# Query projection of an attention kernel: the first product of a query pair one slot earlier, the output projection's slots set around the seven products

## The chip, the cores and the metric

The kernel runs on one core of one Trainium2 chip. The time is the device time of one execution in microseconds (us), and of several timed runs the median is taken. A separate execution was taken by the profiler; its rows give the durations used below.

The engines are named as in the profile: PE is TensorE (matrix products), PEld its weight loads, DVE is VectorE, ACT is ScalarE, SP issues the DMAs. Each engine runs its own instructions in order, and semaphores hold an instruction until another engine has done its part.

## What is computed

Inputs in bfloat16: x is 2048 x 512, the caches hold 32 heads of 2048 keys and values of 128 each. Cut to what matters:

```
xn = layernorm(x)
q  = (xn @ wq), split into 32 heads of 128
p  = softmax(q @ k_cache^T / sqrt(128)), per head
s  = concat(p @ v_cache) @ wo
g  = silu(mlp(xn))          # two gelu stages, shifts, residual
out = x + s * g
```

The change lies in q and in the last product with wo.

## The kernel before, in words

**Units and slots.** After a head of about 100 us for the MLP, the attention runs as 128 units. A unit u is one head (of a group of 4) with one block of 512 queries, in the order group, query block, head in the group. A unit has 8 slots, one for each two key chunks of 128, so slot n of the program is unit n // 8, slot n % 8. The loop over n (line 921 on) writes the order out by hand. In each slot PE gets

- **S**: two products of 512 columns, scores of two key chunks into one of two PSUM tiles `ps_s` (`s_slot`, line 412). ACT then takes exp of both, 128x1024, into `pT` (line 423, "exp" below). The S of slot n needs the exp of slot n-2, because there are two `ps_s` tiles.
- **PV**: two products of 512 columns, weights times values, for the slot 10 earlier (`pv_slot`), into `ps_o`.
- at most one or two **fillers**: a piece of the output projection or of the next units' queries.

**The output projection.** `wo_slot` gives PE one product of 512 columns (`ps_wo`, "wo" below) for one of the 4 heads of a group; four of them make a tile of 128 tokens, and part 4, `wo_post` (line 544), lets DVE add the tile to `sacc` (line 560 in most units), which frees the one `ps_wo` buffer. The list `at_wo` (line 965) says in which slots of a unit the five parts stand. It holds for units 14 to 123 and depends on u % 4.

**The queries.** Units 16 to 125 get their queries in pairs (v, v+1): the two heads' projections of a query block are made from seven products of half size instead of eight, and sums of them. Each product, numbered 1 to 7, is two matmuls of 256 columns (`product`, line 363; "P1" to "P7" below). The pair v is made during the units v-2 (even, "the even unit") and v-1 ("the odd unit"); there are 55 pairs, with even units 14, 16, ..., 122. Products 1, 6 and 2 share one PSUM bank `ps_q` and stand in the even unit; 7, 5, 4 and 3 stand in the odd unit in the same bank, opened anew. In between:

- `q_take` 0 (line 393): ACT copies product 1 to `tq` right after product 1, in the order of ACT behind the exp of the same slot. P6 writes the other half of the same bank, and its first matmul waits for this copy.
- `q_part` 0 (line 400): DVE adds P6 and the copy. `q_take` 1 (line 393): ACT writes the first quarter of the queries behind P2. `q_part` 1, 2, 3 (lines 403, 405, 407): DVE sums of the odd unit; P4 waits for line 405, and the next pair's P1 needs the bank that line 407 reads last.

The table of lines 892 to 895 sets the slots: each (k, n) puts product k at slot n, counted from the even unit's first slot.

**Other DVE work of a unit**: sums over `pT` (lines 429, 434), folds (438, 442), the row sum from a transposing DMA (472), the division of `ps_o` (496), and in some units sums of weights for the coming pairs (361).

Of the kernel before, what the change touches and what calls it, by code (L numbers as in the profile page):

```python
# [17 lines left out]
def kernel(  # L18
# [296 lines left out]
    def q_mm(u, dcs, tag="xa"):  # L315
        g, qt, hh = units[u]
        if dcs[0] == 0:
            st[u] = dict(psq=psX.tile([P, 512], FP32, tag=tag, name="ps_q"))
        for dc in dcs:
            mm(st[u]["psq"][:], wqs[g * HG + hh][:, dc, :],  # L320
               xnT[:, dc, qt * 512:(qt + 1) * 512], dc == 0, dc == DC - 1)
# [73 lines left out]
    def q_part(v, i):  # L395
        s = sw[v]
        ps, t = s["ps"], lambda: pS.tile([P, 256], FP32, tag="tq", bufs=3, name="tq")
        if i == 0:
            s["u"] = t()
            pin(nc.vector.tensor_tensor(out=s["u"][:], in0=ps[:, 1, :], in1=s["m1"][:], op=ALU.add))  # L400
        elif i == 1:
            s["u3"] = t()
            pin(nc.vector.tensor_tensor(out=s["u3"][:], in0=ps[:, 0, :], in1=s["u"][:], op=ALU.add))
        elif i == 2:
            pin(nc.vector.tensor_tensor(out=s["q"][:, 3, :], in0=ps[:, 1, :], in1=s["u3"][:], op=ALU.add))
        else:
            pin(nc.vector.tensor_tensor(  # L407
                out=s["q"][:, 1:3, :], in0=ps[:], in1=s["u"][:].unsqueeze(1).to_broadcast([P, 2, 256]),
                op=ALU.add))
            del sw[v]  # L410

    def s_slot(u, p):
        g, qt, hh = units[u]
        s = st[u]
        sps = psS.tile([P, 2, 512], FP32, name="ps_s")
        for j in range(2):
            kc = 2 * p + j
            kv = kTs[g * HG + hh].rearrange("d (i p j) -> d i j p", p=P, j=KJ)
            mm(sps[:, j, :], kv[:, kc // KJ, kc % KJ, :], s["qT"][:], True, True)
        if p % 2 == 0:  # L420
            s.setdefault("pT", []).append(pB.tile([P, 4, 512], BF16, tag="pT", bufs=6, name="pT"))
        jj = 2 * (p % 2)
        pin(nc.scalar.activation(  # L423
            out=s["pT"][-1][:, jj:jj + 2, :], in_=sps[:], func=ACT.Exp, scale=SCALE))
# [7 lines left out]
    def add_next(u, i):  # L432
        a = st[u]["acc"]
        pin(nc.vector.tensor_tensor(out=a[:], in0=a[:], in1=st[u]["pT"][i][:], op=ALU.add))  # L434

    def fold(u):
        a = st[u]["acc"]
        pin(nc.vector.tensor_tensor(out=a[:, 0:2, :], in0=a[:, 0:2, :], in1=a[:, 2:4, :], op=ALU.add))  # L438

    def fold_last(u):  # L440
        a = st[u]["acc"]
        pin(nc.vector.tensor_tensor(out=a[:, 0, :], in0=a[:, 0, :], in1=a[:, 1, :], op=ALU.add))  # L442
# [22 lines left out]
    def turn(u):  # L465
        st[u]["tT"] = pB.tile([P, 4, P], BF16, tag="tT", bufs=2, name="tT")
        pin(nc.sync.dma_start_transpose(out=st[u]["tT"][:], in_=st[u]["acc"][:, 0, :]))

    def turned_sums(u):
        s = st[u]  # L470
        sm = s["sm"] = smp.tile([P, 4], FP32, name="sm")
        pin(nc.vector.tensor_reduce(out=sm[:], in_=s["tT"][:], axis=mybir.AxisListType.X, op=ALU.add))  # L472

    def turned_recip(u):
        s = st[u]
        sm = s["sm"]
        rc = smp.tile([P, 4], FP32, name="rc")
        pin(nc.vector.reciprocal(out=rc[:], in_=sm[:]))
        s["dr"] = drp.tile([P, 4], FP32, name="dr")
        pin(nc.sync.dma_start(out=s["dr"][:], in_=rc[:]))  # L480

    def bcast(u):
        st[u]["rb"] = pB.tile([P, 512], FP32, tag="rb", bufs=2, name="rb")
        pin(nc.sync.dma_start(
            out=st[u]["rb"][:], in_=st[u]["dr"][:].rearrange("p j -> (p j)").partition_broadcast(P)))
# [54 lines left out]
    def pay():  # L540
        while owed:
            y_out(*owed.popleft(), nc.sync)
# [317 lines left out]
    def pv_run(n):  # L860
        while pv_at[0] <= n - LAG:
            pv_slot(*divmod(pv_at[0], SPU))
            pv_at[0] += 1

    def norm_queue(u):
        norm(u)
        gg, qq, hh = units[u]
        if hh == HG - 1:
            wo_todo.extend((gg, 4 * qq + ts) for ts in range(4))
            if gg == NG - 1 and qq not in LATE:  # L870
                fin_load(4 * qq)
# [3 lines left out]
    def wo_slot(part, n, each=2, **kw):  # L875
        gg, t = wo_todo[0]
        if part < HG // each:
            wo_mm(gg, t, tuple(range(part * each, (part + 1) * each)), **kw)
            return
        wo_todo.popleft()  # L880
        wo_post(gg, t, n)
        if gg == NG - 1 and t % 4 < 3 and t + 1 not in fin and t // 4 not in LATE:
            fin_load(t + 1)
# [5 lines left out]
    first, third = {}, {}  # L889
    for v in pairs:  # L890
        a = (v - 2) * SPU
        for k, n in ((1, 1), (6, 2), (2, 5), (7, 8), (5, 9), (4, 12), (3, 13)):
            steps[a + n].append((product, v, k))
        for i, n in enumerate((1, 5)):
            steps[a + n].append((q_take, v, i))
        steps[a + 14].append((q_part, v, 3))
        first[v - 2] = v
        third[v - 1] = (v,)

    def fold_at(u):  # L900
        return 1 if u in third else 0

    def run_steps(n, which):
        for fn, v, k in steps.get(n, ()):
            if fn is which:
                fn(v, k)
# [4 lines left out]
    for h in range(HG, H, 2):  # L911
        u = (h // HG) * QT * HG + (-4, -2)[h % HG // 2]
# [8 lines left out]
    for n in range(UB * SPU):  # L921
        u, p = divmod(n, SPU)
        extra = len(wo_todo) > 1 and u in (2 * HG, 2 * HG + 1)
        if p == 0 and wo_box:
            wo_slot(4, n, each=1)
        s_slot(u, p)
        pv_run(n)
        for v, dcs in q_plan.get(n, ()):
            q_mm(v, dcs)
        run_steps(n, product)  # L930
        run_steps(n, q_take)
        if p == 0 and 1 <= u:
            if u - 2 in TURN:
                turned_sums(u - 2)
                turned_recip(u - 2)
            add_next(u - 1, 3)
        if p == 1 and u - 2 in TURN:
            bcast(u - 2)
        if p == fold_at(u) and 1 <= u:
            for v in third.get(u, ()):  # L940
                q_part(v, 1)
            fold(u - 1)
            for v in third.get(u, ()):
                q_part(v, 2)
            if u != UA and u not in first:
                fold_last(u - 1)
        if p == 2 and u in first:
            q_part(first[u], 0)
            fold_last(u - 1)
        if p == 3 and u - 1 in TURN:  # L950
            turn(u - 1)
        if p == 0:
            twice = extra
        if twice and p < 3:
            wo_slot(p, n, tag="xa")
        for v, k in ((u + 1, 3), (u + 2, 7)):
            if p == k and "psq" in st.get(v, ()) and (k == 3) == (v > FIRST):
                q_copy(v)
        if u - 2 in TURN:
            norm_p, sum_p, wo_p, each = 7, 5, 3, 1  # L960
        else:
            norm_p, sum_p, wo_p, each = 4, 5, 4, 1
        at_wo = [wo_p + i for i in range(HG // each + 1)]
        if FIRST - 2 <= u < LAST:
            at_wo = ([0, 3, 4, 6, 7], [0, 2, 3, 6, 7], [3, 4, 5, 6, 7], [0, 2, 3, 6, 7])[u % 4]
        if p == norm_p and 2 <= u and not u - 2 in TURN:
            norm_queue(u - 2)
        if p == sum_p and 1 <= u and u - 1 not in TURN:
            sums(u - 1)
        if p == sum_p + 1 and 1 <= u and u - 1 not in TURN:  # L970
            bcast(u - 1)
        if u == UA and p in (1, 2, 3):
            wo_slot(p - 1, n)
            if p == 3:
                fold_last(u - 1)
        if p in at_wo and wo_todo and pS is not None and (p == at_wo[0] or wo_box):
            wo_slot(at_wo.index(p), n, each=each)
        if p == norm_p and u - 2 in TURN:
            norm_queue(u - 2)
        run_steps(n, q_part)  # L980
        if p == 4:
            add_first(u)
        if p == 6:
            add_next(u, 2)
        pay()
        held_mm(n)
        for fn in todo.pop(n, ()):
            fn()
        if pS is None and not held:
            right.close()  # L990
            pS = right.enter_context(pool("pS", side="right", reuse_waits="tile"))
# [3 lines left out]
    n = UB * SPU  # L995
# [156 lines left out]
```

## Time and profile before

| | |
|---|---|
| timed runs, median of 3 | 1241.74 us (1241.14 to 1241.91) |
| the profiled execution | 1240.9 us |
| its span, first to last instruction | 1239.1 us |
| DVE busy, ACT busy | 1030.3 us, 1112.6 us |
| weight loads busy | 644.2 us |
| granted PE clock | 1.0 over the whole span |

The span is 1.8 us shorter than the profiled execution's own time, which lies 0.84 us under the median of the timed runs. A row of the timeline has start, length, engine, line of the kernel, operation, written and read tiles, sizes and count; a bracket at its end gives the idle time before it and what ended that. Matmuls overlap in the rows (a matmul of 512 columns has 0.38 us, and the next one starts much earlier), so PE is read from one start to the next, not from lengths.

### The profile page before, as it was taken

What the parts mean: (1) busy time and instruction counts of PE and PEld (TensorE: products, weight loads), DVE (VectorE), ACT (ScalarE), POOL (GpSimd) and SP (SyncE); (2) the same over time, 40 slices, a digit from 0 to 9 for tenths busy, and PEclk for the clock granted to TensorE, in tenths of its full rate; (3) what the DMA queues carried; (4) which work ended last, traced back from release to release, by engine and by line L of the source; (5) the groups of instructions that cost most, each with busy time, mean ns of one, the idle gap of its engine ahead of it and who ended that gap; (6) DMA issues with size and microseconds to landing.
All of it is one profiled execution on the core that took longest, in us unless ns stands there. A gap on an engine that the chain in (4) does not pass through costs nothing.

```text
span 1239.1 us, 17537 instructions
## 1 busy us (share of the span) xinstructions
PE 1233.0 (100%) x6267; PEld 644.2 (52%) x6267; DVE 1030.3 (83%) x1647; ACT 1112.6 (90%) x1237; POOL 26.7 (2%) x75
## 2 busy tenths in 40 slices
PE   9999999999999999999999999999999999999998
PEld 6444444455555555555555555555555555555555
DVE  7712778898888888888889888888889999999997
ACT  6345999899999999999999999999999999999996
POOL 5300000000000000000000000000000000000000
PEclk9999999999999999999999999999999999999999
DMA  8760112554334423353243423443345435543332
GB/s 175 171 148 21 31 39 65 98 97 91 66 76 100 109 53 82 86 112 84 57 90 95 111 55 69 100 103 75 71 87 107 102 65 86 103 103 69 77 80 67
DMA packets 244056, 107.75 MB, mean 87 GB/s; under 512 B 194816, under 2 KB 227712, under 8 KB 243968
## 3 DMA queue, kind: packets, MB, share of 16 engines
q1 hardware_dynamic: 243408, 106.17, 41.1%
q8 instruction: 49, 0.80, 0.3%
q14 instruction: 39, 0.32, 0.1%
q10 hardware_dynamic: 560, 0.46, 0.1%
HBM read 67.50 MB, written 2.36 MB: 56 GB/s over the span
## 4 chain that ended last, share of the span: by engine, by line
PE 95%; DVE 3%; DMA 1%; ACT 1%; issue 0%; POOL 0%; DVEq 0%; ACTq 0%
PE ps_s L112 39%; PE ps_o L112 37%; PE ps_q L112 8%; PE ps_wo L112 8%; PE ps_m L112 2%; DVE acc L434 1%; ACT pT L423 1%; DMA rb<-dr 0%; DMA tT<-acc 0%; DVE sm L472 0%; DVE oT L496 0%; DMA xin<-in_A_x_dram 0%; PE ps_oh L112 0%; DMA dr<-rc 0%; DVE y L1014 0%
## 5 line engine op out<-in xcount | busy, mean ns | idle before, releaser
L423 ACT ACTIVATE pT<-ps_s 128x1024 bf16<-128x1024 f32 x1016 | 1019.8, 1025 | 54.4 <-PE ps_s L112 24.8
L112 PE MATMUL ps_s<-qT,kT 128*128 128x512 bf16 (+1 forms) x2064 | 609.0, 377 | 0.0
L112 PE MATMUL ps_o<-pT,vb 128*128 128x512 bf16 x1984 | 589.9, 379 | 0.0
L434 DVE TENSOR_TENSOR acc<-acc,pT 128x2048 bf16<-128x2048 bf16 x254 | 307.0, 1209 | 54.6 <-ACT pT L423 54.1
L112 PEld LDWEIGHTS <-kT 128*128 128x128 bf16 x2064 | 232.7, 113 | 147.4 <-issue 2.4
L112 PEld LDWEIGHTS <-vb 128*128 128x128 bf16 x1984 | 194.0, 98 | 216.9 <-issue 0.3
L429 DVE TENSOR_TENSOR acc<-pT 128x2048 bf16<-128x2048 bf16 x127 | 155.4, 1224 | 43.0 <-ACT pT L423 41.9
L112 PE MATMUL ps_wo<-wo_h,oT 128*128 128x512 bf16 x496 | 186.2, 379 | 0.0
L438 DVE TENSOR_TENSOR acc<-acc 128x1024 bf16<-128x1024 bf16 x127 | 87.4, 688 | 2.5
L496 DVE TENSOR_TENSOR oT<-ps_o,rb 128x512 bf16<-128x512 f32 x127 | 86.6, 682 | 1.5 <-DMA rb<-dr 1.2
L472 DVE TENSOR_REDUCE sm<-tT 128x4 f32<-128x512 bf16 x124 | 83.9, 677 | 2.0 <-DMA tT<-acc 2.0
L112 PEld LDWEIGHTS <-oT 128*128 128x128 bf16 x528 | 59.1, 112 | 49.5 <-issue 0.6
L112 PEld LDWEIGHTS <-wc 128*128 128x128 bf16 x440 | 42.9, 98 | 57.9 <-issue 12.7
L560 DVE TENSOR_TENSOR sacc<-ps_wo,sacc 128x512 f32<-128x512 f32 x96 | 65.7, 684 | 0.0
L112 PEld LDWEIGHTS <-wq_h 128*128 128x128 bf16 x398 | 38.9, 98 | 46.3
L112 PE MATMUL ps_q<-xnT,wq_h 128*128 128x256 bf16 (+1 forms) x288 | 61.1, 298 | 0.4 <-DVE sacc L548 0.4
L407 DVE TENSOR_TENSOR qT<-ps_q,tq 128x512 bf16<-128x512 f32 x55 | 38.0, 692 | 23.7 <-PE ps_q L112 23.5
L442 DVE TENSOR_TENSOR acc<-acc 128x512 bf16<-128x512 bf16 x127 | 53.0, 417 | 0.5
L293 ACT ACTIVATE h2T<-ps_s 128x1024 bf16<-128x1024 f32 x28 | 28.7, 1024 | 25.9 <-PE ps_s L112 25.9
L112 PEld LDWEIGHTS <-w_sb 128*128 128x128 bf16 x368 | 33.6, 98 | 29.6
L112 PE MATMUL ps_s<-xn2T,w_sb 128*128 128x512 bf16 x224 | 48.8, 379 | 0.0
L112 PE MATMUL ps_q<-xs,wc 128*128 128x256 bf16 x246 | 46.8, 271 | 0.0
(102 smaller groups left out, 586.4 us busy)
## 6 DMA issues: line engine op xcount, KB each, us to landing
rb<-dr SPq DMA_DIRECT2D x127, 256.0 KB, 3.9
vb<-in_A_v_cache_dram SPq DMA_DIRECT2D x62, 256.0 KB, 3.0
wq_h<-in_A_wq_dram SPq DMA_DIRECT2D x32, 128.0 KB, 3.1
wo_h<-in_A_wo_dram SPq DMA_DIRECT2D x32, 128.0 KB, 2.7
w_sb<-in_B_w_dram SPq DMA_DIRECT2D x8, 256.0 KB, 5.1
kT<-in_A_k_cache_dram SPq DMA_TRANSPOSE x128, 2.8
xl<-in_A_x_dram SPq DMA_DIRECT2D x16, 128.0 KB, 3.0
dr<-rc SPq DMA_DIRECT2D x127, 2.0 KB, 1.4
```

The costliest lines, as they stand in the source:

```text
L112: pin(nc.tensor.matmul(out=out, lhsT=lhsT, rhs=rhs, start=start, stop=stop, **kw))
L293: pin(nc.scalar.activation(out=h2[c, f][:], in_=ps[:], func=ACT.Gelu_apprx_tanh))
L407: pin(nc.vector.tensor_tensor(out=s["q"][:, 1:3, :], in0=ps[:], in1=s["u"][:].unsqueeze(1).to_broadcast([P, 2, 256]), op=ALU.add))
L423: pin(nc.scalar.activation(out=s["pT"][-1][:, jj:jj + 2, :], in_=sps[:], func=ACT.Exp, scale=SCALE))
L429: pin(nc.vector.tensor_tensor(out=s["acc"][:], in0=s["pT"][0][:], in1=s["pT"][1][:], op=ALU.add))
L434: pin(nc.vector.tensor_tensor(out=a[:], in0=a[:], in1=st[u]["pT"][i][:], op=ALU.add))
L438: pin(nc.vector.tensor_tensor(out=a[:, 0:2, :], in0=a[:, 0:2, :], in1=a[:, 2:4, :], op=ALU.add))
L442: pin(nc.vector.tensor_tensor(out=a[:, 0, :], in0=a[:, 0, :], in1=a[:, 1, :], op=ALU.add))
L472: pin(nc.vector.tensor_reduce(out=sm[:], in_=s["tT"][:], axis=mybir.AxisListType.X, op=ALU.add))
L496: pin(nc.vector.tensor_tensor(out=to, in0=o, in1=rb, op=ALU.mult))
L560: pin(nc.vector.tensor_tensor(out=sa, in0=ps[:], in1=sa, op=ALU.add))
```

## The change

Two lines of tables and one of the copy's places:

```diff
-        for k, n in ((1, 1), (6, 2), (2, 5), (7, 8), (5, 9), (4, 12), (3, 13)):
+        for k, n in ((1, 0), (6, 2), (2, 5), (7, 8), (5, 9), (4, 12), (3, 13)):
             steps[a + n].append((product, v, k))
-        for i, n in enumerate((1, 5)):
+        for i, n in enumerate((0, 5)):
             steps[a + n].append((q_take, v, i))
...
         if FIRST - 2 <= u < LAST:
-            at_wo = ([0, 3, 4, 6, 7], [0, 2, 3, 6, 7], [3, 4, 5, 6, 7], [0, 2, 3, 6, 7])[u % 4]
+            at_wo = ([1, 3, 4, 6, 7], [0, 2, 3, 6, 7])[u % 2]
```

P1 and its copy go from slot 1 to slot 0 of each even unit. The wo products of the even units, before in slots 0, 3, 4, 6 (u % 4 = 0) or 3, 4, 5, 6 (u % 4 = 2), now stand in 1, 3, 4, 6 in both. The odd units keep theirs. Every instruction that was there is there still: PE, DVE, ACT and SP have as many as before, and DVE and SP have them in the same order.

PE in an even unit with u % 4 = 2, from P1's second matmul on; `ps_q<-xnT,wq_h` is P1, `ps_q<-xs,wc` is P6, `ps_s` S, `ps_o` PV. Before:

```order
L112 LDWEIGHTS wq_h
L112 MATMUL ps_q<-xnT,wq_h 128x256
L112 LDWEIGHTS kT
L112 MATMUL ps_s<-qT,kT 128x512 [waits Activation_49]
L112 LDWEIGHTS kT
L112 MATMUL ps_s<-qT,kT 128x512
L112 LDWEIGHTS vb
L112 MATMUL ps_o<-pT,vb 128x512 [waits DVE_49]
L112 LDWEIGHTS vb
L112 MATMUL ps_o<-pT,vb 128x512
L112 LDWEIGHTS wc
L112 MATMUL ps_q<-xs,wc 128x256 [waits Activation_49]
```

Now, from the same matmul on (P1 stands in slot 0, and the rows end in slot 1):

```order
L112 LDWEIGHTS wq_h
L112 MATMUL ps_q<-xnT,wq_h 128x256
L112 LDWEIGHTS kT
L112 MATMUL ps_s<-qT,kT 128x512 [waits Activation_49]
L112 LDWEIGHTS kT
L112 MATMUL ps_s<-qT,kT 128x512
L112 LDWEIGHTS vb
L112 MATMUL ps_o<-pT,vb 128x512
L112 LDWEIGHTS vb
L112 MATMUL ps_o<-pT,vb 128x512
L112 LDWEIGHTS oT
L112 MATMUL ps_wo<-wo_h,oT 128x512 [waits DVE_49]
```

One S and one PV stood between P1 and P6, whose wait is on ACT; now a wo product with a wait on DVE follows at that place, and P6 comes a whole slot later, behind another S and PV.

PE in an even unit with u % 4 = 0, from the second PV matmul of slot 0 on. Before:

```order
L112 MATMUL ps_o<-pT,vb 128x512
L112 LDWEIGHTS oT
L112 MATMUL ps_wo<-wo_h,oT 128x512 [waits DVE_49]
L112 LDWEIGHTS kT
L112 MATMUL ps_s<-qT,kT 128x512 [waits Activation_49]
```

Now:

```order
L112 MATMUL ps_o<-pT,vb 128x512
L112 LDWEIGHTS wq_h [waits DMAHW6_49]
L112 MATMUL ps_q<-xnT,wq_h 128x256
L112 LDWEIGHTS wq_h
L112 MATMUL ps_q<-xnT,wq_h 128x256
L112 LDWEIGHTS kT
L112 MATMUL ps_s<-qT,kT 128x512 [waits Activation_49]
```

The wo product that waited for DVE in slot 0 has made room for P1, and stands in slot 1.

ACT from the exps ahead of the first pair to those behind it; `tq<-ps_q` is the copy of P1, `qT<-ps_q` that of P2. Before:

```order
L423 ACTIVATE pT<-ps_s 128x1024 x50
L393 ACTIVATE tq<-ps_q 128x256
L423 ACTIVATE pT<-ps_s 128x1024 x4
L393 ACTIVATE qT<-ps_q 128x256
L423 ACTIVATE pT<-ps_s 128x1024 x12
```

Now:

```order
L423 ACTIVATE pT<-ps_s 128x1024 x49
L393 ACTIVATE tq<-ps_q 128x256
L423 ACTIVATE pT<-ps_s 128x1024 x5
L393 ACTIVATE qT<-ps_q 128x256
L423 ACTIVATE pT<-ps_s 128x1024 x11
```

The copy of P1 has moved ahead of one exp: it follows the exp of slot 0 instead of that of slot 1.

## Prediction

> **What bounds the kernel now.** I read the page's busy times first, then the chain, then a table of busy time by stretch, then the timeline of two even units.
>
> ```profile
> PE 1233.0 (100%) x6267; PEld 644.2 (52%) x6267; DVE 1030.3 (83%) x1647; ACT 1112.6 (90%) x1237; POOL 26.7 (2%) x75
> ...
> PE 95%; DVE 3%; DMA 1%; ACT 1%; issue 0%; POOL 0%; DVEq 0%; ACTq 0%
> ```
>
> The chain that ended last is PE in 95%. But a busy PE can hide waits, since its rows overlap. So I count. The next fence holds two stretches of 16 units each (units 38 to 53 and 54 to 69), with PE, PEld, DVE, ACT and POOL busy, then clock, DMA share and GB/s; then come PE's and ACT's rows around slot 0 to 3 of unit 56 (u % 4 = 0), and of unit 58 (u % 4 = 2).
>
> ```profile
> 452.80:590.10 137.30, 137.30 (x690) 72.13 (x689) 118.48 (x186) 131.39 (x145) 0.00 (x0) 1.00 0.39 85
> 590.10:727.40 137.30, 137.30 (x690) 71.98 (x689) 118.49 (x186) 131.61 (x145) 0.00 (x0) 1.00 0.38 85
> ```
>
> ```profile
> 607.28 0.59 PE L112 MATMUL ps_s<-qT,kT 128*128 128x512 bf16 x2
> ...
> 608.15 0.38 PE L112 MATMUL ps_wo<-wo_h,oT 128*128 128x512 bf16 x1
> ...
> 609.23 0.38 PE L112 MATMUL ps_q<-xnT,wq_h 128*128 128x256 bf16 x2
> ...
> 609.45 0.59 PE L112 MATMUL ps_s<-qT,kT 128*128 128x512 bf16 x2
> ...
> 609.88 0.59 PE L112 MATMUL ps_o<-pT,vb 128*128 128x512 bf16 x2
> 609.92 0.38 ACT L393 ACTIVATE tq<-ps_q 128x256 f32<-128x256 f32 x1
> ...
> 610.35 0.38 PE L112 MATMUL ps_q<-xs,wc 128*128 128x256 bf16 x2
> ...
> 610.56 0.59 PE L112 MATMUL ps_s<-qT,kT 128*128 128x512 bf16 x2
> ```
>
> ```profile
> 624.39 0.59 PE L112 MATMUL ps_s<-qT,kT 128*128 128x512 bf16 x2
> 624.82 0.59 PE L112 MATMUL ps_o<-pT,vb 128*128 128x512 bf16 x2
> 625.25 0.59 PE L112 MATMUL ps_s<-qT,kT 128*128 128x512 bf16 x2
> ...
> 626.33 0.59 PE L112 MATMUL ps_s<-qT,kT 128*128 128x512 bf16 x2
> 626.76 0.59 PE L112 MATMUL ps_o<-pT,vb 128*128 128x512 bf16 x2
> 627.34 0.38 PE L112 MATMUL ps_q<-xs,wc 128*128 128x256 bf16 x2
> ```
>
> A product (two matmuls of 256 columns) takes 0.22 us from its start to the next one's (609.23 to 609.45). Between the S at 610.56 and that at 626.33 stand 15 slots with 67 matmuls of 512 columns and six products: (15.77 - 6 x 0.22) / 67 = 0.2157 us each. At that pace 16 units, with 576 such matmuls and 56 products, need 124.2 + 12.3 = 136.6 us, of the 137.3 they take. **PE streams 99.5% of the time, and 0.7 us in 16 units is all it waits.** At the same rate the 110 units of the pairs wait 4.8 us.
>
> Where? Two PV matmuls take 0.43 us. In unit 56 P6 should start at 609.88 + 0.43 = 610.31 and starts at 610.35; in unit 58 it should start at 627.19 and starts at 627.34. So P6 comes 0.04 and 0.15 us late, four units lose 0.19, and 16 lose 0.76, which is the 0.7 above. What it waits for is the copy:
>
> ```profile
> 607.97 1.02 ACT L423 ACTIVATE pT<-ps_s 128x1024 bf16<-128x1024 f32 x1
> ...
> 625.08 1.02 ACT L423 ACTIVATE pT<-ps_s 128x1024 bf16<-128x1024 f32 x1
> 625.98 1.03 ACT L423 ACTIVATE pT<-ps_s 128x1024 bf16<-128x1024 f32 x1
> ...
> 626.89 0.40 ACT L393 ACTIVATE tq<-ps_q 128x256 f32<-128x256 f32 x1
> 627.15 1.05 ACT L423 ACTIVATE pT<-ps_s 128x1024 bf16<-128x1024 f32 x1
> ```
>
> The copies end at 610.30 and 627.29, and P6 starts 0.05 us behind each. In unit 58 the exps of slots 0 and 1 and the copy follow each other at 0.90 and 0.91 us: ACT is behind there, because slot 7 of the odd unit and slot 0 hold no filler, and PE has run ahead of it.
>
> **The change part by part.** None of the moved instructions issues a DMA, and SP and POOL keep their order, so PE and ACT are what is left to follow, and DVE where they wait for it. *P1 and its copy, one slot earlier.* Take unit 58. Its S is at 624.39 and its PV at 624.82, so P1 stands at 625.25 and its last row ends by 625.63 (0.38). The exp of slot 0 still starts at 625.08, and ACT is free for the copy 0.90 later, at 625.98, with P1 done. The copy ends at 626.38. P6 now has P1, S, PV, a wo product, S and PV in front of it after slot 0's PV: 625.25 + 0.22 + 0.86 + 0.22 + 0.86 = 627.41. **The copy is done 1.03 us before P6 wants it**, where it was 0.10 too late for an unhindered start. In unit 56, where the exp of slot 0 starts at 607.97, the same working gives a copy at 608.87, done by 609.25, and P6 at 610.31. So the wait goes in all 55 pairs: 28 x 0.15 + 27 x 0.04 = 5.3 us (even units 14, 18, ..., 122 and 16, ..., 120).
>
> What is late next? The exp of slot 1 now stands behind the copy: an exp starts 0.26 after a copy (626.89 to 627.15), so at 626.24 in unit 58, and ends at 627.27; S of slot 3 needs it, and stands at 627.41 + 0.22 = 627.63. In unit 56 that exp starts at 609.13 and ends at 610.16, for an S at 610.31 + 0.22 = 610.53. That leaves over 0.3 us.
>
> ```profile
> 617.04 0.59 PE L112 MATMUL ps_s<-qT,kT 128*128 128x512 bf16 x2
> ...
> 617.67 9.34 ACT L423 ACTIVATE pT<-ps_s 128x1024 bf16<-128x1024 f32 x9 [0.21 <-PE ps_s L112]
> ```
>
> An exp that finds ACT free starts 0.2 us behind the 0.43 of its S (617.04 + 0.63). In unit 58 the exp of slot 2 can so start at 626.55 + 0.63 = 627.18, and ACT is free for it at 626.24 + 0.90 = 627.14: ACT has caught up within one slot, and what follows stands as before.
>
> *P1 and its bank.* P1 needs the bank that line 407 reads last for the pair before.
>
> ```profile
> 605.54 0.69 DVE L407 TENSOR_TENSOR qT<-ps_q,tq 128x512 bf16<-128x512 f32 x1 [0.53 <-PE ps_q L112]
> ...
> 607.28 0.68 DVE L560 TENSOR_TENSOR sacc<-ps_wo,sacc 128x512 f32<-128x512 f32 x1
> ```
>
> It ends at 606.23, P1 moves to 608.15: 1.9 us to spare, and DVE had waited 0.53 us for PE there, so it isn't DVE that is late. Nothing.
>
> *The wo products.* In units with u % 4 = 0 slots 0 and 1 swap fillers. In the others the fillers of slots 1 to 6, with two in slot 5 and none in slot 0, become one each in slots 0 to 6. Every S behind has at least the room it had, because PE's longest run without a filler gets shorter. The order shows a new wait on DVE at the wo of slot 1: `ps_wo` must have been read by line 560. That row ends at 607.96, 0.68 us after unit 56's first S, and the wo now stands 1.08 + 0.86 = 1.94 behind it. Behind the waiting wo stand all of PE's work and with it ACT, so a late line 560 would cost in full; 1.2 us are to spare. It even saves something: in every 16th unit DVE is later by a weight sum (line 361), and the wo of slot 0 has to wait.
>
> ```profile
> 675.91 0.28 DVE L361 TENSOR_TENSOR wc<-wq_h,wc 128x256 bf16<-128x256 bf16 x1
> 676.11 0.68 DVE L560 TENSOR_TENSOR sacc<-ps_wo,sacc 128x512 f32<-128x512 f32 x1
> ```
>
> ```profile
> 676.34 0.59 PE L112 MATMUL ps_o<-pT,vb 128*128 128x512 bf16 x2
> 676.85 0.38 PE L112 MATMUL ps_wo<-wo_h,oT 128*128 128x512 bf16 x1
> ```
>
> The wo should start at 676.77 and starts at 676.85, behind line 560's end at 676.79. By the slots of the weight sums, units 16, 32, ..., 112 make seven such places, 7 x 0.08 = 0.5 us, and in slot 1 it is gone.
>
> *What is given back.* The view of waits for the pairs' stretch (us in total, times, longest) has two places where DVE itself is late for P4:
>
> ```profile
> ACT pT L423 <- PE ps_s L112: 13.8, 60, 0.6
> ...
> PE ps_q L112 <- DVE qT L405: 0.6, 2, 0.4
> ```
>
> There PE only waits longer for what it saved just before, 0.2 us together as an estimate (a saving of 0.15 and of 0.04, nearly all).
>
> **Sum.** From the rows 5.3 + 0.5 = 5.8 us, from the stretches 4.8 (0.7 is known to 0.1, so 4.1 to 5.5). I take 5.5, nearer to the rows, which see each place, less 0.2: **5.3 us**. The profiled execution would go from 1240.9 to 1235.6 us, its span from 1239.1 to 1233.8. The median of the timed runs lies 0.84 above the profiled one, so I forecast 1241.74 - 5.3 = **1236.4 us**.
>
> **The rivals.** *ScalarE sets the pace* (no change, 1241.7 us). An exp lasts 1.025 us and the copies 0.39 and 0.38:
>
> ```profile
> L423 ACT ACTIVATE pT<-ps_s 128x1024 bf16<-128x1024 f32 x881 | 885.4, 1025 | 41.0 <-PE ps_s L112 13.8
> L393 ACT ACTIVATE tq<-ps_q 128x256 f32<-128x256 f32 x55 | 21.5, 391 | 0.0
> L393 ACT ACTIVATE qT<-ps_q 128x256 bf16<-128x256 f32 x55 | 20.8, 377 | 0.0
> ```
>
> 16 x 1.025 + 0.77 = 17.17 us a pair, and a pair takes 137.30 / 8 = 17.16. If these lengths were what ACT needs, PE would only wait elsewhere. Against it: queued exps start 0.90 us apart and 0.26 behind a copy, so a pair needs 16 x 0.90 + 0.5 = 14.9, and ACT waited for PE 60 times. Chance 0.08. [...]
>
> *The change doesn't do what it says* (no change, 1241.7 us): P6's wait on ACT is still there in the order, and if it were for a later exp than the copy it would stay. P6's start 0.05 us behind the copy's end in both units speaks against it. Chance 0.03.
>
> *The wait moves to slot 3 and grows* (slower). The copy now delays the exp of slot 1, and S of slot 3 needs that exp. It decides from the point where the exp is later by 0.3 us more than worked out. Were it 0.2 us past that in each pair, 55 x 0.2 = 11 us would stand against 5.4: 1247.3 us. For it: ACT is behind PE just there. Against it: even with no overlap at all (exp 1.025, copy 0.39, exp 1.025 from 625.08) the exp would end at 627.52, before the S at 627.63. Chance 0.05, with 0.01 for anything else that is slower.
>
> **How the numbers follow.** Forecast 0.83, no change 0.11, slower 0.06. A measurement of this kernel can tell about 0.2%, 2.5 us, from no change; the forecast lies beyond that, so faster 0.83, same 0.11, slower 0.06. The low end takes all 5.8 us, the 0.6 of P4's waits too, and 0.4 for the spread of the runs: 1235.0. The high end takes the stretches' least, 4.1, less 0.8 given back and 0.4 spread: 2.9 us, 1238.8. The rivals, 0.17, lie outside.
>
> **What would show it.** Right: P6 starts 0.43 us behind its PV in both kinds of even unit; 16 units take 136.6 us; the copy starts 0.9 us behind the exp of slot 0; the exp of slot 1 starts some 0.15 us later behind its S than the others do. Wrong: S of slot 3 starting late, ACT's idle time before exps gone while the pair still takes 17.16 us, or a wo in slot 1 starting behind a line 560.

## The result and the profile after

The changed kernel takes **1237.29 us** (median of 6 runs, 1236.24 to 1237.56) against 1241.83 us for the kernel before beside it (6 runs): a ratio of 0.9962, 95% interval 0.9949 to 0.9975, or 4.5 us gained. The forecast was 1236.4 us, 5.3 us gained, within 1235.0 to 1238.8. The profiled execution took 1236.51 us, its span is 1234.7 us (4.4 less than before).

The page after has PE's busy time 4.7 us lower and DVE's unchanged; PE's share of the chain is 94% (95% before):

```profile
PE 1228.3 (99%) x6267; PEld 644.5 (52%) x6267; DVE 1030.3 (83%) x1647; ACT 1105.8 (90%) x1237; POOL 26.7 (2%) x75
...
PE 94%; DVE 3%; DMA 2%; ACT 1%; issue 0%; POOL 0%; DVEq 0%; ACTq 0%
```

The two stretches of 16 units (38 to 53, 54 to 69), columns as before:

```profile
451.70:588.30 136.60, 136.60 (x690) 72.10 (x689) 118.69 (x186) 130.50 (x145) 0.00 (x0) 1.00 0.41 86
588.30:724.80 136.50, 136.50 (x689) 72.08 (x688) 118.48 (x185) 130.61 (x145) 0.00 (x0) 1.00 0.41 86
```

They took 137.30 before and were forecast at 136.6, the pace at which PE only streams. Slots 0 to 3 of unit 58 in the timeline after:

```profile
623.12 1.02 ACT L423 ACTIVATE pT<-ps_s 128x1024 bf16<-128x1024 f32 x1
623.29 0.38 PE L112 MATMUL ps_q<-xnT,wq_h 128*128 128x256 bf16 x2
...
624.02 0.39 ACT L393 ACTIVATE tq<-ps_q 128x256 f32<-128x256 f32 x1
624.28 1.04 ACT L423 ACTIVATE pT<-ps_s 128x1024 bf16<-128x1024 f32 x1
...
625.02 0.59 PE L112 MATMUL ps_o<-pT,vb 128*128 128x512 bf16 x2
625.45 0.38 PE L112 MATMUL ps_q<-xs,wc 128*128 128x256 bf16 x2
625.67 0.59 PE L112 MATMUL ps_s<-qT,kT 128*128 128x512 bf16 x2
```

The copy starts 0.90 us behind the exp of slot 0 and ends at 624.41. P6, at 625.45, follows its PV by 0.43: it no longer waits, 1.04 us to spare (forecast 1.03). The exp of slot 1 ends at 625.32, 0.35 ahead of the S of slot 3.

What became longer is P4's wait for DVE. Views of waits over the pairs' stretch, after:

```profile
ACT pT L423 <- PE ps_s L112: 14.8, 63, 0.8
...
PE ps_q L112 <- DVE qT L405: 1.1, 3, 0.6
```

Before, the last row had 0.6 us in 2 waits. Such a row counts only gaps that show: a PV row is drawn 0.16 us longer (0.59) than its step (0.43), so 0.16 is missing from every wait, and short ones are missing whole. From start to start P4 waited 1.07 us before and 1.92 after.

### The profile page after: what moved, and what is told of

It reads as the page before. It is cut to its first block, busy times and chain, and to the rows that moved or that the text cites. A ratio compares the mean times of both kernels' runs of the same rounds, so it can differ in the third digit from the quotient of the medians.

```text
span 1234.7 us, 17537 instructions
## 1 busy us (share of the span) xinstructions
PE 1228.3 (99%) x6267; PEld 644.5 (52%) x6267; DVE 1030.3 (83%) x1647; ACT 1105.8 (90%) x1237; POOL 26.7 (2%) x75
## 4 chain that ended last, share of the span: by engine, by line
PE 94%; DVE 3%; DMA 2%; ACT 1%; issue 0%; POOL 0%; DVEq 0%; ACTq 0%
PE ps_s L112 39%; PE ps_o L112 37%; PE ps_wo L112 8%; PE ps_q L112 8%; PE ps_m L112 2%; DVE acc L434 1%; DMA tT<-acc 1%; ACT pT L423 1%; DMA rb<-dr 0%; DVE sm L472 0%; DVE oT L496 0%; DMA xin<-in_A_x_dram 0%; DMA dr<-rc 0%; PE ps_oh L112 0%; DVE acc L438 0%
```

## The experiments

All times below come from the same reading: **stretch** is the time from the S of unit 14 to the S of unit 124 in the profiled execution, **P6** and **P4** what these waited in it, counted from start to start. A step longer by just 0.216 us, where a matmul record is missing (120 of 6267 in some of the traces), is no wait and isn't counted. Two numbers are two executions of the same kernel. Each ratio is to runs of the kernel before in the same session, whose medians were 1241.83, 1241.06, 1241.40 and 1241.36 us, so ratios compare better than times.

| kernel | median of runs, us | ratio (95%) | stretch, us | P6 | P4 |
|---|---|---|---|---|---|
| before | | | 945.45; 945.60 | 4.8; 4.9 | 1.07; 1.16 |
| changed | 1237.29; 1236.47 | 0.9962 (0.9949-0.9975); 0.9962 (0.9948-0.9975) | 940.87; 940.97 | 0; 0 | 1.92; 2.02 |
| P1 alone | 1236.46 | 0.9965 (0.9953-0.9978) | 941.80 | 0 | 2.69 |
| wo alone | 1239.30 | 0.9985 (0.9977-0.9994) | 943.32 | 2.0 | 1.50 |
| copy late | 1238.20 | 0.9976 (0.9967-0.9986) | 941.77 | 2.1 | 0.84 |
| P4 later | 1237.61 | 0.9971 (0.9961-0.9981) | 942.03 | 0 | 0.05 |
| lines 526, 531 later | 1235.40; 1235.47 | 0.9952 (0.9939-0.9964); 0.9955 (0.9942-0.9967) | 939.92; 939.98 | 0; 0 | 0.81; 0.98 |
| one copy more | 1236.84 | 0.9966 (0.9954-0.9978) | 940.88 | 0 | 2.13 |
| two copies more | 1248.93 | 1.0061 (1.0045-1.0076) | 953.54 | 0 | 1.52 |
| bare pair | 1239.76 | 0.9988 (0.9979-0.9997) | 943.93 | 0 | 2.5 |

Theory A: the gain is P6's wait for the copy, which went because the copy stands one exp earlier. Rival B: it comes from fillers that are spread evenly over the slots. For what was given back, theory C: P4 waits for a late line 405; rival D: DVE paces that stretch, and a wait there only moves.

**P1 and its copy alone**, wo as before:

```
-        for k, n in ((1, 1), (6, 2), ...
+        for k, n in ((1, 0), (6, 2), ...
-        for i, n in enumerate((1, 5)):
+        for i, n in enumerate((0, 5)):
```

> P1 and its copy in slot 0, the wo products in the slots of the kernel before. Theory A (P6 no longer waits, because the copy stands one exp earlier): P6 starts 0.43 us behind its PV in all even units, the copy being done more than 0.7 us ahead; the wo of slot 0 in units with u % 4 = 0 stands behind P1 and so finds line 560 done. Nearly the whole gain: 1237.3 us, within 0.7. Theory B (the gain comes from one filler in each of the slots 0 to 6 instead of none in one slot and two in another): the fillers are still uneven, more so in units with u % 4 = 0, and little of the gain is left: 1241 us or more. The exp of slot 1 has less room here where slot 1 holds no filler (about 0.1 us before the S of slot 3), so by A a few hundredths may be lost in each pair, 1 to 2 us in all, if that room is smaller than worked out.

1236.46 us: the whole gain with fillers as uneven as before, as A has it and B doesn't. **wo alone**, P1 and copy as before:

```
-            at_wo = ([0, 3, 4, 6, 7], [0, 2, 3, 6, 7], [3, 4, 5, 6, 7], [0, 2, 3, 6, 7])[u % 4]
+            at_wo = ([0, 3, 4, 6, 7], [0, 2, 3, 6, 7])[u % 2]
```

> P1 and its copy in slot 1 as before, the wo products of all even units in slots 0, 3, 4 and 6, so units with u % 4 = 2 get the pattern of those with u % 4 = 0. Theory A: P6 still waits for the copy, but in the formerly worse units by 0.04 us instead of 0.15, because slot 0 holds a filler and ACT is less behind: 28 x 0.11 = 3.1 us gained, less some 0.5 for seven more wo products in slot 0 that wait for line 560, and less what VectorE takes back at P4: about 1239.5 us, with P6 0.04 us late in all 55 even units. Theory B: fillers as even as in the changed kernel but for the order of slots 0 and 1, so the whole gain, 1237.3 us.

1239.30 us. P6's waits of 0.15 us became 0.04, since the wo in slot 0 keeps PE from running ahead of ACT, but none went: 2.0 of 4.8 us stayed. In seven more units the wo of slot 0 now waits for line 560 (1.0 us in all, 0.5 before). So either half of the change gets part of the gain; only the earlier copy gets all. **The copy back behind the exp of slot 1**, all else as changed:

```
-        for i, n in enumerate((0, 5)):
+        for i, n in enumerate((1, 5)):
```

> The changed kernel with the copy of P1 put back behind the exp of slot 1; P1 stays in slot 0 and the wo products in their new slots. Theory A: the copy starts behind the exp of slot 1 and ends about when P6 wants to start; P6 waits 0.03 to 0.04 us in each of the 55 pairs, 1.7 to 2.2 us of the gain are lost: about 1239.2 us. Theory B, and a theory by which P1's own place is what counts: as the changed kernel, 1237.3 us, P6 unhindered.

P6 waits again, in all 55 pairs. Unit 56 in its timeline:

```profile
607.73 1.02 ACT L423 ACTIVATE pT<-ps_s 128x1024 bf16<-128x1024 f32 x1
608.65 0.38 ACT L393 ACTIVATE tq<-ps_q 128x256 f32<-128x256 f32 x1
...
608.61 0.59 PE L112 MATMUL ps_o<-pT,vb 128*128 128x512 bf16 x2
609.08 0.38 PE L112 MATMUL ps_q<-xs,wc 128*128 128x256 bf16 x2
```

P6 starts 0.05 us behind the copy's end (609.03) and 0.04 later than PV allows; 55 x 0.04 = 2.2. The fillers are spread as in the changed kernel, so spreading them doesn't by itself end the wait, and B is out as the cause. The time, 1238.20, lies a microsecond under A's figure, and in the profiled execution P4 waited 1.1 us less than in the changed kernel. By the medians alone the two kernels can't be told apart, since their intervals overlap; the counted waits tell them apart.

**P4 one slot later**, into slot 13 with P3, the odd unit's wo moved to make room:

```
-        ... (5, 9), (4, 12), (3, 13)):
+        ... (5, 9), (4, 13), (3, 13)):
...
-            at_wo = ([1, 3, 4, 6, 7], [0, 2, 3, 6, 7])[u % 2]
+            at_wo = ([1, 3, 4, 6, 7], [0, 2, 3, 4, 7])[u % 2]
```

> The changed kernel with P4 in slot 5 of the odd unit, next to P3, instead of slot 4, and the wo product of slot 6 in slot 4 instead. Theory C (what the change gave back is PE waiting for line 405 of VectorE at P4, 1.9 us in six late odd units, and VectorE itself, with its extra sums there, is what is late): P4 then has 1.08 us more room than the largest wait of 0.72, all these waits go, 1.9 us: about 1235.4 us. Rival D (VectorE is the pace of that stretch as a whole, so the wait only moves to the next place where PE needs it, the division at line 496 or line 407): 1237.3 us, with the same 1.9 us of waiting found at other PE rows.

P4's waits went, as C has it, and yet nothing was gained: now the first S of every even unit comes 0.04 us late (2.4 us in all). One wait did move on, as D has it: a wo product in unit 111 comes 0.38 us late, behind line 553 of DVE. **The bare pair** moves the wo alone, P4 stays in slot 12:

```
-            at_wo = ([1, 3, 4, 6, 7], [0, 2, 3, 6, 7])[u % 2]
+            at_wo = ([1, 3, 4, 6, 7], [0, 2, 3, 4, 7])[u % 2]
```

> The changed kernel with the odd units' output projection in slots 0, 2, 3, 4, 7 instead of 0, 2, 3, 6, 7; P4 stays in slot 12. Two slots in a row, 14 and 15, then mostly have no filler and are 0.863 us long, while queued exps start 0.90 to 0.92 us apart. If that is what made the first S of each even unit wait 0.04 us when P4 stood in slot 13: the same wait here, 55 x 0.04 = 2.2 us, 1239.5 us. Rival (that wait came from P3 and P4 in one slot): no wait at that S, 1237.3 us.

It has the same wait at the same S, 55 x 0.04 = 2.2 us, at 1239.76 us. So the two slots 6 and 7 without a filler make it, not P4. But the reason expected for it, exps that queue 0.90 to 0.92 us apart, is wrong: ACT was idle just there. The timeline with P4 later, ahead of unit 56, and then the views of waits with P4 later and with the bare pair:

```profile
604.38 0.59 PE L112 MATMUL ps_s<-qT,kT 128*128 128x512 bf16 x2
...
605.07 1.94 ACT L423 ACTIVATE pT<-ps_s 128x1024 bf16<-128x1024 f32 x2 [0.34 <-PE ps_s L112]
...
605.68 0.59 PE L112 MATMUL ps_o<-pT,vb 128*128 128x512 bf16 x2
606.15 0.59 PE L112 MATMUL ps_s<-qT,kT 128*128 128x512 bf16 x2
```

```profile
ACT pT L423 <- PE ps_s L112: 29.1, 104, 0.6
```

```profile
ACT pT L423 <- PE ps_s L112: 29.7, 111, 1.1
```

From an S at 604.38 to its exp are 0.69 us, the exp takes 1.02, and the S that gets the same `ps_s` tile starts some 0.05 later: a round of 1.77 us, though ACT had been idle for 0.34. Two slots without a filler take 2 x 0.863 = 1.73. The 0.04 between them is the wait. ACT waited for S 104 and 111 times, where it had waited 63 times in the changed kernel.

Not every such pair of slots waits. In the kernel before, slot 7 ahead of unit 58 and slot 0 of unit 58 had no filler either:

```profile
623.52 0.59 PE L112 MATMUL ps_s<-qT,kT 128*128 128x512 bf16 x2
...
624.16 1.02 ACT L423 ACTIVATE pT<-ps_s 128x1024 bf16<-128x1024 f32 x1
```

Here the exp starts 0.63 us behind its S, and the S of slot 1, at 625.25, follows at 1.73 without a wait. In the traces of the kernel before, the changed one, P4 later and the bare pair, exps that find ACT idle start 0.63 behind their S where they wait for PE alone, and 0.69 in the slots 2 and 6, where the exp also waits for a semaphore of ACT itself and the wait for PE is an instruction of its own ahead of it (three in each trace start 0.97 behind). That second wait thus goes with the 0.06 us that are missing in slot 6; no run takes it away to show it.

**The margin at slot 3.** Small extra copies (of a constant, unused) behind the copy of slot 0: one, then two, of which the second waits for the first. The cut shows the version with one:

```
     def q_take(...)
...
+        for _ in range(1 if i == 0 else 0):
+            pin(nc.scalar.activation(out=warm[:], in_=ident[:], func=ACT.Identity))
```

> The changed kernel with one more small ScalarE copy (128x128, some 0.16 us) behind the copy of slot 0, so that the exp of slot 1 ends 0.16 us later in each pair. The prediction's margin of 0.3 us in front of S of slot 3: hidden, no PE wait at S of slot 3, 1237.3 us. Rival (ScalarE sets the pace of the pair): 55 x 0.16 = 8.8 us more, 1246.1 us.

> The same with two small copies, the second waiting for the first, some 0.49 us in each pair. By the margin (0.34 us in the changed kernel's trace between the end of the exp of slot 1 and S of slot 3): S of slot 3 waits 0.15 us in each pair, 55 x 0.15 = 8.2 us, 1245.5 us. If the margin is larger than the trace says: 1237.3 us. If ScalarE sets the pace: 55 x 0.49 = 27 us, 1264 us.

Unit 58 with one, then with two (the exp is line 425 here, the extra copy 395):

```profile
624.12 0.39 ACT L393 ACTIVATE tq<-ps_q 128x256 f32<-128x256 f32 x1
624.38 0.32 ACT L395 ACTIVATE warm<-ident 128x128 bf16<-128x128 bf16 x1
624.58 1.95 ACT L425 ACTIVATE pT<-ps_s 128x1024 bf16<-128x1024 f32 x2
...
625.55 0.38 PE L112 MATMUL ps_q<-xs,wc 128*128 128x256 bf16 x2
625.77 0.59 PE L112 MATMUL ps_s<-qT,kT 128*128 128x512 bf16 x2
```

```profile
629.07 0.39 ACT L393 ACTIVATE tq<-ps_q 128x256 f32<-128x256 f32 x1
629.33 0.66 ACT L395 ACTIVATE warm<-ident 128x128 bf16<-128x128 bf16 x2
629.90 1.92 ACT L425 ACTIVATE pT<-ps_s 128x1024 bf16<-128x1024 f32 x2
...
630.50 0.38 PE L112 MATMUL ps_q<-xs,wc 128*128 128x256 bf16 x2
630.96 0.59 PE L112 MATMUL ps_s<-qT,kT 128*128 128x512 bf16 x2
```

One copy puts the exp of slot 1 0.46 us behind the copy's start instead of 0.26, 0.20 later, and S stays 0.22 behind P6: hidden, 1236.84 us. Two put it 0.83 behind, 0.57 later, and S starts 0.46 behind P6: a wait of 0.24, so the margin is 0.33. In 55 pairs that makes 13.4 us at this S alone, and the stretch is 12.7 longer. ScalarE doesn't set the pace (8.8 us for one copy were expected by that), but past a third of a microsecond this edge costs in full. The second copy cost 0.37, more than the expectation had, hence 1248.93 instead of 1245.5 us. The Trainium skill, ScalarE: Activation LUTs, "What ACT_TABLE_LOAD costs", gives 186 ns + 0.833 ns a column for an activation with immediate scale and bias, less 93 ns between back-to-back ones; for 128 columns that is an estimate of 0.20 us, as the first copy cost.

**What was given back.** In unit 97 before, and after:

```profile
961.12 0.69 DVE L472 TENSOR_REDUCE sm<-tT 128x4 f32<-128x512 bf16 x1 [0.78 <-DMA tT<-acc]
...
963.04 0.68 DVE L526 SCALAR_TENSOR_TENSOR sacc<-sacc,xall 128x512 f32<-128x512 f32 x1
...
964.58 0.42 DVE L405 TENSOR_TENSOR qT<-ps_q,tq 128x256 bf16<-128x256 f32 x1
965.05 0.38 PE L112 MATMUL ps_q<-xnT,wc 128*128 128x256 bf16 x2 [0.24 <-DVE qT L405]
```

```profile
957.43 0.69 DVE L472 TENSOR_REDUCE sm<-tT 128x4 f32<-128x512 bf16 x1 [1.09 <-DMA tT<-acc]
...
959.36 0.69 DVE L526 SCALAR_TENSOR_TENSOR sacc<-sacc,xall 128x512 f32<-128x512 f32 x1
...
960.89 0.42 DVE L405 TENSOR_TENSOR qT<-ps_q,tq 128x256 bf16<-128x256 f32 x1
961.37 0.38 PE L112 MATMUL ps_q<-xnT,wc 128*128 128x256 bf16 x2 [0.56 <-DVE qT L405]
```

DVE waits for the transposing DMA, then does an extra sum (line 526, which finishes an output tile early and stands in few units), and line 405 comes too late for P4. **Lines 526 and 531 four slots later**:

```
-            k = n + SPU * (t - 4 * LATE[0]) + 1
+            k = n + SPU * (t - 4 * LATE[0]) + 5
```

> The changed kernel with the late scale and add of a finished tile (lines 526 and 531) four slots later, so that they no longer stand ahead of line 405 on VectorE. Theory C (what is given back is P4 waiting for line 405, which is late where a late transposing DMA and line 526 fall together): P4's waits in the units 97, 103 and 109, 1.6 of 1.93 us, go; those of 0.11 us in units 119 to 123, behind line 569, stay: 1237.3 - 1.6 = 1235.7 us. Rival D (VectorE sets the pace there, a wait only moves on): 1237.3 us, with the 1.6 us at another of PE's instructions.

The same unit in its timeline:

```profile
957.27 0.69 DVE L472 TENSOR_REDUCE sm<-tT 128x4 f32<-128x512 bf16 x1 [0.77 <-DMA tT<-acc]
...
960.13 0.42 DVE L405 TENSOR_TENSOR qT<-ps_q,tq 128x256 bf16<-128x256 f32 x1
960.82 0.38 PE L112 MATMUL ps_q<-xnT,wc 128*128 128x256 bf16 x2
961.93 0.68 DVE L526 SCALAR_TENSOR_TENSOR sacc<-sacc,xall 128x512 f32<-128x512 f32 x1
```

Line 405 ends at 960.55, ahead of P4, though the DMA still makes DVE wait 0.77, as long as in the kernel before (0.78), where P4 was late: C. P4's waits in the units 97, 103 and 109 are gone. The edit moves more than the two sums, though: loads of the tiles' x rows (line 522) go later with them, and in unit 103 DVE no longer waits for the transposing DMA at all, so there the sum alone isn't shown to be the cause. And 0.6 us stands at P4 in unit 121, where the division waits for its DMA:

```profile
1162.56 0.69 DVE L496 TENSOR_TENSOR oT<-ps_o,rb 128x512 bf16<-128x512 f32 x1 [0.55 <-DMA rb<-dr]
...
1166.49 0.38 PE L112 MATMUL ps_q<-xnT,wc 128*128 128x256 bf16 x2 [0.43 <-DVE qT L405]
```

It is there in both executions of this version. The changed kernel lost 0.11 us there in one execution and 0.45 in the other, so whether a part of it is a wait that moved on, as D has it, stays open. Of the 1.6 us, 0.95 and 0.99 are left as gain in the stretch.

Last, whether P4's waits come from the change or differ from execution to execution: both kernels profiled again, with this version beside them.

> The changed kernel once more, profiled a second time. If P4's waits (1.9 us in its first profile, against 1.1 us before) are given back by the change, they are the same 1.9 us, in the units 97, 103, 109, 119, 121 and 123. If they hang on when DMAs land, and so differ between executions, other units wait, and the sum lies anywhere between 1.1 and 2.7 us, as it does over the kernels so far that leave P4 in slot 12. 1236.9 us either way.

> The kernel before, profiled a second time: P4's waits 1.1 us again, in the units 97, 109 and 121, if the change sets them; other units and another sum if DMA landings do.

> The version with lines 526 and 531 four slots later, beside the changed kernel on one chip: 1.1 us less than that if its first profile (P4's waits 0.8 us against 1.9) is typical, 1235.6 us; no difference if the waits move about between executions.

The sums repeat (before 1.07 and 1.16, changed 1.92 and 2.02), though the units differ: before it was 97, 109, 121 and then 103, 109, 121. So the change gives back 0.86 us, by two executions of each. On one chip the changed kernel took 1236.47 us (1235.78 to 1237.04) and the version with the later sums 1235.47 (1235.24 to 1235.75), 1.0 less, where 1.1 less was expected. It is the fastest of the versions run, though the intervals of their ratios overlap.

## Why the prediction was right, and where its sum was off

- *P6's wait goes* (5.3 us): right in place and mechanism, a little too large. Start to start it was 4.8 us before and is 0 after. The later copy brings 2.1 of it back, the earlier copy alone removes it all.
- *wo in slot 0 behind line 560* (0.5): right, 0.5 before and none after.
- *Given back* (0.2): **mis-sized**, 0.86. I took PE's wait as what it had saved just before, 0.15 and 0.04 in two places. But the size is set by how late DVE is: in units 97 and 103 by the transposing DMA ahead of line 526, in unit 109 by the division's DMA ahead of it (1.6 us together), in units 119, 121 and 123 where line 569 stands (0.11 each). That was six units instead of three, with up to 0.72 us. The term was also read from a view that showed 0.6 us where 1.07 were waited. With 0.9 in the place of 0.2 the sum is 5.5 - 0.9 = 4.6, and the stretch measured 945.45 - 940.87 = 4.6. The 5.5 lay between two estimates; counted, it is 4.8 + 0.5 and 0.2 of two small waits (a PV in unit 122, an S in unit 74) that went too, so its agreement is in part luck.
- *ScalarE sets the pace* (a rival): wrong. One copy more in each pair cost nothing, and queued exps with rows of 1.025 us start 0.90 apart.
- *The wait moves to slot 3* (a rival): it didn't, but mechanism and point were right: it decides from 0.33 us (0.3 forecast), and 0.24 past that cost 12.7 us of stretch.
- *The median lies 0.84 us above the profiled run*: 0.78 after.

What stays open: why the transposing DMA lets DVE wait longer in the changed kernel (in unit 97 1.09 and 1.24 us in its two executions, 0.78 and 0.37 before). Over the kernels with P4 in slot 12 and the early sums, P4's waits lie between 0.84 and 2.69 us; the four lowest, up to 1.50, are the kernel before, its second profile, the late copy and wo alone, in all of which PE is held at P6 in every pair. That PE's running ahead makes DVE's lateness show is a guess from this.

## What to carry to other kernels

Where an engine is shown 100% busy, count from start to start at a pace taken from a stretch that nothing holds up: waits of 0.04 us, 55 times over, show there and in no list of waits. A short operation of another engine that the busy engine waits for belongs behind the earliest work that it can follow, and the margin of what it pushes back has to be counted first. A saving is handed on at the points where some other engine is late now and then, and these have to be sized by how late that engine gets, not by the saving.

## What the hardware did that I had not expected

- Two `ps_s` tiles make a round: S to exp, exp, exp to S. It took 0.69 + 1.02 + 0.05 = 1.77 us from slot 6 on, and there two slots of 0.863 us wait 0.04, with ACT idle for 0.34 us just before. From slot 7 on, where S to exp is 0.63, two such slots pass without a wait.
- An exp that waits for two semaphores started 0.06 us later behind its S (0.69) than one that waits for one (0.63).
- A 128x128 copy is drawn 0.32 us long and cost the exp behind it 0.20; a second one that waits for the first cost 0.37.
